# Longformer attention fused with a feed-forward layer: units 16 to 127 issued by one function, attention two units later, twelve more units by seven products of halves

## The chip, the core and the metric

The kernel runs on one core of a Trainium2 chip. The metric is the device time of one execution in microseconds (us), as the median of several runs; less is better. TensorE (PE) multiplies matrices and writes PSUM; VectorE (DVE), ScalarE (ACT) and GpSimd (POOL) do elementwise work, and the SyncE queue (SP) issues the DMAs. Each of these engines takes its instructions in the order in which they stand in its queue.

## The reference

There are 8 batches with 8 heads; each head has 512 local and 32 global tokens of 64 numbers. Local tokens attend to a band of 32 to each side and to the global tokens; global tokens attend to all. The result, 4608 rows of 512, goes through a feed-forward layer with 2048 hidden values:

```
s_l = concat(scale * q_l @ k_g.T, where(|i - j| <= 32, scale * q_l @ k_l.T, -1e9))
out_l = softmax(s_l) @ concat(v_g, v_l)
out_g = softmax(scale * q_g @ concat(k_g, k_l).T) @ concat(v_g, v_l)
x = concat(out_g, out_l).reshape(4608, 512)
h = x @ w_in                                            # 512 -> 2048
y = (max(h, 0) + alpha * min(h, 0)) @ w_out             # 2048 -> 512
```

The attention's inputs are float32; w_in and w_out are float64, and the kernel decodes their bits.

## The kernel before, in words

**Units.** The feed-forward layer is cut into units. Unit T = 16 G + f takes batch G (512 rows; G = 8 is the batch of all global rows) and 128 hidden values, f = 0 to 15. Its first half (`f1`, line 804) makes h, 128 hidden by 512 rows, in a PSUM bank `h_ps`; the slopes follow on DVE and ACT (`slopes`, line 903, or `negatives` and `add_slopes`, lines 887 and 892); the result is split into an upper part gh (ACT) and a lower part gl (POOL). Its second half (`f2`, line 919) adds 12 products of 128x512 to the four banks o0 to o3. `f2` of a unit is issued two units later (LAG = 2). Each number is the sum of two parts (xh and xl, two planes of a weight), and three of the four products of parts are made.

**Plain and fast units.** A plain unit's h takes 12 matmuls over 512 columns. `f1_fast` (line 831) makes two units together by seven products of halves, each of 6 matmuls over 256 columns: 4 products in the even unit (of the x parts b11, t1, t2, t3, in this order), 3 in the odd one (b22, b21, t4). It needs sums of quarters of the weights (`weight_sums`, line 396: per pair of units q, 6 DVE subtractions and additions, 3 ACT copies, 3 POOL subtractions into s24, s3 and a quarter of the weights), and sums of quarters of x (`x_sums`, line 735, called by `prepare`, line 791, at the places that X_STEPS names): for b11, t1, t2, t3, b22, b21 and t4 an upper part by ACT and a lower part by DVE or POOL, and between them subtractions `less` (line 732) in x_raw. In `product` (line 825) the third matmul of the first half reads the lower part of x.

**Attention.** It runs beside the units in quarters of four for each pair of heads P (four pairs are a batch). In the quarter s = 0 PE makes the local scores (`s_ps`), DVE masks and reduces them, ACT takes the exponentials, POOL multiplies by the inverse sums (`p`). In s = 1 and s = 3 DVE transposes and the SP queue sends p through a scratch buffer in DRAM. In s = 2 PE makes the weighted values of the pair before (`o_ps`, then `g_ps`) and the global scores (in `g_ps`), ACT copies the values to x_raw, and the global softmax follows. DVE clears a part of the g_ps bank (MEMSET, line 560) before PE may write it. The x sums of a batch need its four pairs.

**Stages.** `begin` (line 996) issues units 0 to 15, the decoding of the weights and the first pairs by a planner. Units 16 to 29 (`slow_unit`, line 1171) leave the order on DVE, ACT and POOL to the framework's scheduler; units 30 and 31 (`border_units`) and 32 to 127 (`fast_unit`, line 1216) keep the order in which they are written. Units 0 to 31 and 128 to 143 are plain, 32 to 127 fast. On PE all is in written order. In `fast_unit` a unit t has the quarter s = (t + 22) mod 4.

Of the kernel before, what the change touches and what calls it, by code (L numbers as in the profile page):

```python
# [34 lines left out]
HP = 50  # L35
NPRE = 19
LAG = 2
# [265 lines left out]
def longformer_ffn(ctx: ExitStack, tc: tile.TileContext, qk, v, w, alpha, out):  # L303
# [82 lines left out]
    def load_out_weights(T):  # L386
        wos[T] = wpool.tile([128, 2, 512], F32R, tag="w", name="wo")
        sync.dma_start(wos[T].bitcast(F32), wod[T % NF])
# [342 lines left out]

    def less(o, a, b):
        vec.tensor_tensor(o, a, b, op=ALU.subtract)

    def x_sums(G, step):
        if step == 0:
            upper(G, "b11", b11)
            lower(G, "b11", b11, vec)
            less(b11, b12, b11)
        if step == 1:  # L740
            less(b12, b22, b12)
        if step == 2:
            upper(G, "t1", b11)
            upper(G, "t3", b12)
            lower(G, "t1", b11, vec)
        if step == 3:
            less(b11, b22, b11)
            upper(G, "t2", b11)
# [13 lines left out]
    def x_last(step):  # L762

        G = NB - 1
        if step == 0:
            upper(G, "b11", b11)
            lower(G, "b11", b11, vec)
            less(b11, b12, b11)
            less(b12, b22, b12)
        if step == 1:  # L770
            spare("t2")
            upper(G, "t1", b11)
            upper(G, "t3", b12)
            lower(G, "t1", b11, vec)
        if step == 2:
            less(b11, b22, b11)
            lower(G, "t3", b12, vec)
        if step == 3:
            upper(G, "t2", b11)
            upper(G, "b22", b22)  # L780
            upper(G, "b21", b21)
            lower(G, "t2", b11, vec)
        if step == 4:
            lower(G, "b22", b22, pool)
            lower(G, "b21", b21, vec)
        if step == 5:
            less(b21, b21, b11)
            upper(G, "t4", b21)
            lower(G, "t4", b21, pool)

    def prepare(t, at):
        G, f = divmod(t, NF)
        if f:
            G += 1
        if G == NB - 1 and (f, at) in LAST_STEPS:
            x_last(LAST_STEPS.index((f, at)))
        if G * NF not in FAST or (f, at) not in X_STEPS:
            return
        if G < NB - 1:
            x_sums(G, X_STEPS.index((f, at)))  # L800
# [24 lines left out]
    def product(dst, w, x, start):  # L825
        for c in range(2):
            for j, e in ((0, 0), (1, 0), (0, 1)):
                matmul(dst, w[:, j, 128 * c : 128 * c + 128], x[e][:, 256 * c : 256 * c + 256], start=start, stop=not start, skip_group_check=True)
                start = False

    def f1_fast(T):
        G, f = divmod(T, NF)
        q = f // 2
# [49 lines left out]
        if f == NF - 1:  # L883
            return added, both
        return even, odd

# [5 lines left out]
    def add_slopes(T, g, h):  # L892
        f = T % NF
# [9 lines left out]
    def slopes(T, h, n):  # L903
        f = T % NF
# [73 lines left out]

    def values(P, first):
        last = gpart.pop(P)  # L980
        if live(P - 1):
            ob = bank(first, "o_ps")
            pv_all(P - 1, ob, last)
        if live(P):
            global_scores(P)
        if live(P - 1):
            pv_out(P - 1, ob, last)
# [127 lines left out]
    def attn(u, where):  # L1115
        P, s = divmod(u, 4)
        if not (live(P) or live(P - 1)):
            return
        if (s, where) == (0, "pre") and live(P):
            local_scores(P)  # L1120
        if s < 2 and where == "pre" and live(P):
            part = softmax(P, s)
            part["red"]()
            part["ex"]()
            tails.extend(part[k] for k in ("rza", "rzr", "nm"))
        if where == "mid":
            while tails:
                tails.pop(0)()
        if (s, where) == (2, "mid"):
            gpart[P] = global_bank(P)  # L1130
            values(P, "s")
            if live(P):
                load_v(P)
        if not live(P):
            return
        if (s, where) == (2, "post"):
            global_softmax(P)
            if live(P + 2):
                load_qk(P + 2)
        if P >= NRAW:  # L1140
            if (s, where) == (2, "pre") and (P, 0) not in scratch:
                transpose_q(P, 0)
            if u == NPRE + 2 * NF + len(CATCH) - 1 and where == "post":
                transpose_q(P, 0)
            if (s, where) == (3, "pre") and P > 8:
                fetch_pt(P, 0)
                transpose_q(P, 1)
            if (s, where) == (3, "post") and P > 8:
                fetch_pt(P, 1)

    tails = []

    begin()
    pin_sync[0] = False
    steps = [[] for t in range(NT + LAG)]
    u = NPRE + NF
    for t in range(NF, NT + LAG):
        steps[t] = [u, u + 1] if t in CATCH else [u]
        u = steps[t][-1] + 1

    def attention(t, at):
# [189 lines left out]
```

## Time and profile before

| | us |
|---|---|
| median of three runs | 886.47 (884.85 to 890.36) |
| the profiled execution, as timed | 887.61 |
| its span (first to last instruction) | 885.8 |
| around the span | 1.8 |
| PE busy in the span | 866.2 |
| DVE, ACT, POOL busy | 616.3, 392.7, 323.9 |

The times in the rows below count from the start of the span. A row of the timeline gives the start, how long it lasts until its last instruction ends, engine, line, operation, the tiles (out<-in), shapes, the number of instructions, and in brackets idle time before it with what ended it. A matmul's end is modelled; starts of matmuls that follow each other give their pace.

### The profile page before, as it was taken

The numbers are of one execution on the slowest core, as the hardware profiler recorded it, in microseconds if no ns is written. First come the engines' busy times: TensorE is split into PE (matmuls) and PEld (weight loads), VectorE is DVE, ScalarE is ACT, GpSimd is POOL, SyncE is SP. The second block draws the span as 40 slices with busy tenths as digits, with TensorE's granted clock in tenths as the row PEclk, the third lists the DMA queues.
The fourth block names the chain that finished last, engine by engine and source line by source line (L and its number), as shares of the span: only waits on it lengthen the run. The fifth ranks groups of instructions, "written<-read, shape, count | busy, mean of one in ns | idle before, by whom it ended". The sixth has DMA issues, their size and how long they took to land.

```text
span 885.8 us, 22467 instructions
## 1 busy us (share of the span) xinstructions
PE 866.2 (98%) x8678; PEld 751.2 (85%) x8678; DVE 616.3 (70%) x1690; ACT 392.7 (44%) x1162; POOL 323.9 (37%) x281
## 2 busy tenths in 40 slices
PE   7799999999999999999999999999999999999998
PEld 5677777878888888888898888888898898889898
DVE  7999999976767667666676667666676656455432
ACT  7898885544444334432354334432354324211221
POOL 4455443655434332423243332423243323222222
PEclk9999999999999999999999999999999999999999
DMA  9879997977457766776657666776657553645630
GB/s 357 343 256 387 335 336 251 324 247 236 152 180 220 250 214 220 263 241 232 211 173 254 211 215 217 255 250 231 212 184 250 173 185 95 215 168 169 220 134 25
DMA packets 80906, 201.23 MB, mean 227 GB/s; under 512 B 21280, under 2 KB 41248, under 8 KB 77088
## 3 DMA queue, kind: packets, MB, share of 16 engines
q1 hardware_dynamic: 80800, 199.80, 66.1%
q8 instruction: 69, 1.13, 0.5%
q14 instruction: 37, 0.30, 0.1%
HBM read 160.96 MB, written 38.80 MB: 226 GB/s over the span
## 4 chain that ended last, share of the span: by engine, by line
PE 73%; DVE 14%; DMA 6%; ACT 4%; issue 2%; POOL 1%; SPq 1%; DVEq 0%; ACTq 0%; POOLq 0%
PE o L323 34%; PE h_ps L323 30%; PE o_ps L323 4%; PE s_ps L323 3%; DVE wt L294 2%; PE g_ps L323 2%; DVE wsum L294 2%; DVE p L294 2%; DVE g L294 2%; ACT p L294 2%; DVE wraw L294 1%; DMA pt<-scratch 1%; DMA scratch<-p 1%; DMA v<-in_v_dram 1%; DMA wa<-wt 1%
## 5 line engine op out<-in xcount | busy, mean ns | idle before, releaser
L294 POOL TENSOR_TENSOR gl<-g,gh 128x512 fp32r<-128x512 f32 (+1 forms) x128 | 161.4, 1263 | 368.0 <-ACT gh L294 270.4
L323 PE MATMUL o<-gh,wo 128*128 128x512 f32 (+1 forms) x1024 | 244.4, 380 | 0.0
L323 PE MATMUL h_ps<-xh,wt 128*128 128x256 f32 (+1 forms) x1024 | 222.4, 310 | 2.2 <-DVE g L294 1.3
L294 ACT CAST gh<-g 128x512 fp32r<-128x512 f32 (+1 forms) x144 | 85.9, 597 | 289.0 <-DVE g L294 288.3
L323 PEld LDWEIGHTS o<-gh,wo 128*128 128x128 f32 x1024 | 176.7, 188 | 32.1 <-issue 0.4
L323 PEld LDWEIGHTS h_ps<-xh,wt 128*128 128x128 f32 x1024 | 166.2, 188 | 20.5 <-issue 4.0
L323 PE MATMUL h_ps<-xl,wt 128*128 128x256 f32 (+1 forms) x512 | 157.4, 307 | 0.0
L323 PE MATMUL o<-gl,wo 128*128 128x512 f32 (+1 forms) x512 | 131.2, 377 | 0.0
L294 DVE TENSOR_SCALAR g<-h_ps,alpha_sb 128x512 f32<-128x512 f32 (+1 forms) x116 | 82.5, 712 | 39.0 <-PE h_ps L323 33.6
L323 PEld LDWEIGHTS o<-gl,wo 128*128 128x128 f32 x512 | 92.8, 188 | 18.5
L294 POOL TENSOR_TENSOR p<-p,rz 128x512 f32<-128x512 f32 x64 | 70.7, 1121 | 96.2 <-DVE rz L294 93.4
L323 PEld LDWEIGHTS h_ps<-xl,wt 128*128 128x128 f32 x512 | 96.1, 188 | 5.1
L294 DVE TENSOR_TENSOR h_ps<-u,h_ps 128x256 f32<-128x256 f32 x144 | 61.1, 425 | 50.6 <-PE h_ps L323 48.7
L294 ACT ACTIVATE p<-p,mn 128x128 f32<-128x128 f32 x224 | 86.9, 396 | 5.1 <-DVE mn L294 4.9
L323 PE MATMUL h_ps<-xh,s 128*128 128x256 f32 x480 | 88.6, 280 | 0.4 <-DVE h_ps L294 0.2
L294 DVE TENSOR_TENSOR u<-u,h_ps 128x256 f32<-128x256 f32 x96 | 40.3, 420 | 57.0 <-PE h_ps L323 36.7
L323 PEld LDWEIGHTS h_ps<-xh,s 128*128 128x128 f32 x480 | 75.9, 188 | 4.3 <-ACT xe L294 0.7
L294 DVE SCALAR_TENSOR_TENSOR g<-h_ps,g 128x512 f32<-128x512 f32 (+1 forms) x116 | 75.9, 654 | 3.8
L323 PE MATMUL h_ps<-xl,s 128*128 128x256 f32 x240 | 67.1, 279 | 0.0
L294 POOL TENSOR_TENSOR wt<-wt,wr 128x512 int32<-128x512 int32 x32 | 45.4, 1423 | 52.4 <-DVE wt L294 35.0
L323 PEld LDWEIGHTS o_ps<-pt,v 128*64 128x64 f32 x1600 | 49.7, 138 | 8.2 <-issue 2.7
L323 PE MATMUL o_ps<-pt,v 128*64 128x32 f32 (+1 forms) x1600 | 53.5, 223 | 1.7 <-DMA pt<-scratch 1.0
(102 smaller groups left out, 1137.1 us busy)
## 6 DMA issues: line engine op xcount, KB each, us to landing
wo<-wo SPq DMA_DIRECT2D x128, 512.0 KB, 4.3
v<-in_v_dram SPq DMA_DIRECT2D x29, 1024.0 KB, 5.4
qk<-in_qk_dram SPq DMA_DIRECT2D x30, 672.0 KB, 7.0
wraw<-in_w_dram SPq DMA_DIRECT2D x32, 512.0 KB, 8.4
scratch<-p SPq DMA_DIRECT2D x112, 128.0 KB, 2.8
pt<-scratch SPq DMA_DIRECT2D x28, 512.0 KB, 5.7
wo<-wt SPq DMA_DIRECT2D x16, 512.0 KB, 7.1
out_dram<-ost SPq DMA_DIRECT2D x32, 256.0 KB, 3.5
```

The costliest lines, as they stand in the source:

```text
L294: ins = op(*a, **k)
L323: ins = nc.tensor.matmul(*a, **k)
```

## The change

Units 16 to 127 are now all issued by one function, `unit`, with the order on DVE, ACT and POOL as it is written; `slow_unit`, `border_units`, the queue of attention steps and `x_last` are gone. The quarter of unit t is s = (t + 20) mod 4, so that attention stands two units further behind: scores are in units 0, 4, 8 and 12 of a batch (before: 2, 6, 10, 14), weighted values in 2, 6, 10 and 14 (before: 0, 4, 8, 12). Units 16 to 19 are plain, 20 to 31 now fast. The x parts of batch 1 are made in units 16, 17 and 20 (`x_second`), with the upper and lower parts of batch 1's x that were there already used as b11, b21, b22 and t4's store. Weight sums are made in two parts, in the units that FIRSTS and RESTS name; pairs q = 0 and 1 come last, and batch 2 takes its hidden values in a turned order (`hidden`). Odd units of batches 1 and 2 use `added` and `both` (negatives on ACT). The last batch uses the same `x_sums` as the others.

```diff
-FAST = range(2 * NF, NB * NF)
-CATCH = (16, 23, 30)
+PLAIN = NF + 4
+FIRSTS = {17: 2, 19: 3, 21: 4, 23: 5, 25: 6, 27: 7, 33: 0, 37: 1}
+RESTS = {18: 2, 20: 3, 22: 4, 24: 5, 26: 6, 28: 7, 34: 0, 38: 1}
 X_STEPS = [(12, "mid"), (13, "post"), (14, "post"), (15, "pre"), (15, "mid"), (15, "post"), (0, "mid")]
-LAST_STEPS = [(12, "post"), (13, "mid"), (13, "post"), (14, "mid"), (14, "post"), (15, "mid")]
+LATE = 4
+    def x_second(step):
+        if step == 0:
+            less(b11, b12, b11)
+            less(b12, b22, b12)
+            upper(1, "t1", b11)
+            upper(1, "t3", b12)
+        if step == 1:
+            ...
+            lower(1, "t1", b11, vec)
+            less(b11, b22, b11)
+            upper(1, "t2", b11)
+            lower(1, "t3", b12, vec)
+            less(b21, b21, b11)
+            lower(1, "t2", b11, vec)
+        if step == 2:
+            for c in range(2):
+                act.copy(xs[1, "t4"](0, c), x_raw[:, 2 + c, 0:256])
+                pool.tensor_tensor(xs[1, "t4"](1, c), x_raw[:, 2 + c, 0:256], xs[1, "t4"](0, c).bitcast(F32), op=ALU.subtract)
     def x_sums(G, step):
         if step == 0:
             upper(G, "b11", b11)
             lower(G, "b11", b11, vec)
+        if step == 1:
             less(b11, b12, b11)
-        if step == 1:
-            less(b12, b22, b12)
+            one_half(b12, b22, b12, 0)
         if step == 2:
             upper(G, "t1", b11)
+            lower(G, "t1", b11, vec)
+            one_half(b12, b22, b12, 1)
+            less(b11, b22, b11)
+        if step == 3:
+            if G == NB - 1:
+                spare("t2")
             upper(G, "t3", b12)
-            lower(G, "t1", b11, vec)
-        if step == 3:
-            less(b11, b22, b11)
             upper(G, "t2", b11)
         if step == 4:
             lower(G, "t2", b11, vec)
+    def hidden(T):
+        G, f = divmod(T, NF)
+        return (f + LATE) % NF if G == 2 else f
-        if f == NF - 1:
+        if f == NF - 1 or G in (1, 2):
             return added, both
-    def fast_unit(t):
-        P, s = divmod(steps[t][0], 4)
+    def unit(t):
+        P, s = divmod(t + 20, 4)
...
-        one, two = f1_fast(t)
+        one, two = f1_plain(t) if t < PLAIN else f1_fast(t)
...
+            if t == NF:
+                x_second(0)
+            if t == PLAIN:
+                x_second(2)
+            if t in RESTS and s == 0:
+                late.pop(RESTS[t])()
             prepare(t, "mid")
...
+            if t == NF + 1:
+                x_second(1)
             prepare(t, "mid")
             if s == 1 and live(P):
                 transpose_q(P, 0)
...
+            if t in FIRSTS:
+                late[FIRSTS[t]] = weight_sums(FIRSTS[t], True)
         f2(t - LAG, 0)
...
         f2(t - LAG, 1)
+        if t in RESTS and s == 2:
+            late.pop(RESTS[t])()
-        if NF <= t < 2 * NF and t % 2 == 0:
-            store_a21((t - NF) // 2)
+        if NF <= t < NF + NF // 2:
+            store_a21((2, 3, 4, 5, 6, 7, 0, 1)[t - NF])
```

Three places of the order that results. The first is PE where batch 3 begins, after the product of t3 in unit 48 (s_2854 before, s_3984 after are tiles of weight sums). Before, the weighted values of a pair follow it:

```order
L323 MATMUL h_ps<-xh,s_2854 128x256 x2
L323 MATMUL h_ps<-xl,s_2854 128x256
L323 MATMUL o_ps<-pt,v 64x32 x2
L323 MATMUL o_ps<-pt,v 64x2x32 x2
L323 MATMUL o_ps<-pt,v 64x32 x4
L323 MATMUL o_ps<-pt,v 64x2x32 x2
```

After, the out-projection follows, and then unit 49 (s_3983):

```order
L322 MATMUL h_ps<-xh,s_3984 128x256 x2
L322 MATMUL h_ps<-xl,s_3984 128x256
L322 MATMUL o_3945<-gh,wo 128x512 x2
L322 MATMUL o_3946<-gh,wo 128x512 x2
L322 MATMUL o_3947<-gh,wo 128x512 x2
L322 MATMUL o_3948<-gh,wo 128x512 x2
L322 MATMUL o_3945<-gl,wo 128x512
L322 MATMUL o_3946<-gl,wo 128x512
L322 MATMUL o_3947<-gl,wo 128x512
L322 MATMUL o_3948<-gl,wo 128x512
L322 MATMUL h_ps<-xh,s_3983 128x256 x2
L322 MATMUL h_ps<-xl,s_3983 128x256
```

The weighted values moved out of the stretch between the even and the odd products of the first pair of units of a batch; the scores moved in ahead of that stretch.

The second is DVE at the same border. Before, from the softmax of unit 46 (rz) to the subtraction that makes t4 in unit 48 (the last row), with the lower parts of t3, t2, b21 among the xl rows and the MEMSET for unit 48:

```order
L294 RECIPROCAL rz<-rz 128x4 x2
L294 TENSOR_TENSOR xl<-x_raw,xh 128x512
L294 TENSOR_TENSOR h_ps<-u,h_ps 128x256 x2
L294 TENSOR_TENSOR x_raw<-x_raw 128x2x256
L294 SCALAR_TENSOR_TENSOR g<-g,beta_sb,h_ps 128x512 x2
L294 TENSOR_TENSOR xl<-x_raw,xh 128x512 x2
L294 STREAM_TRANSPOSE p<-p 128x512 x2
L294 MEMSET g_ps 64x32
L294 TENSOR_TENSOR u<-u,h_ps 128x256 x2
L294 TENSOR_TENSOR h_ps<-u,h_ps 128x256
L294 TENSOR_TENSOR xl<-x_raw,xh 128x512
L294 TENSOR_TENSOR x_raw<-x_raw 128x2x256
```

After, the stretch of units 46 and 47, from the global softmax to the lower parts of t2 and t3:

```order
L293 TENSOR_TENSOR x_glb<-x_glb,g_ps 128x32
L293 TENSOR_REDUCE gm<-g_ps 128x1
L293 TENSOR_SCALAR gm<-gm 64x1 x2
L293 TENSOR_SCALAR gz<-gz 64x1 x2
L293 RECIPROCAL gz<-gz 128x1
L293 TENSOR_TENSOR xl<-x_raw,xh 128x512
L293 TENSOR_TENSOR x_raw<-x_raw 128x256
L293 TENSOR_TENSOR x_raw<-x_raw 128x2x256
L293 STREAM_TRANSPOSE sg_sb<-sg_sb 128x384
L293 TENSOR_TENSOR h_ps<-u,h_ps 128x256 x2
L293 SCALAR_TENSOR_TENSOR g<-g,beta_sb,h_ps 128x512 x2
L293 TENSOR_TENSOR xl<-x_raw,xh 128x512 x2
```

Eight masked reductions of the scores of unit 48 follow, and then:

```order
L293 ISA p,mn<-s_ps,mask 128x4x32
L293 ISA mn 128x1
L293 TENSOR_TENSOR u<-u,h_ps 128x256 x2
L293 TENSOR_TENSOR h_ps<-u,h_ps 128x256
L293 TENSOR_TENSOR xl<-x_raw,xh 128x512
L293 TENSOR_TENSOR x_raw<-x_raw 128x2x256
L293 RECIPROCAL rz<-rz 128x4 x2
```

The global softmax stands ahead of the lower part of t1, and eight reductions stand between the lower part of t3 and the sums u; the subtraction for t4 stands behind them.

The third is DVE in units 16 to 18. Before, the MEMSET for unit 18 stands among the weight sums of one pair (wsum) in unit 16 or 17 (the g rows are the slopes):

```order
L294 TENSOR_TENSOR wsum<-wsum 128x256
L294 MEMSET g_ps 64x32
L294 TENSOR_TENSOR wsum<-wsum 128x256 x3
L294 TENSOR_SCALAR g<-h_ps,alpha_sb 128x512
L294 TENSOR_TENSOR wsum<-wt 128x512 x2
L294 SCALAR_TENSOR_TENSOR g<-h_ps,g 128x512
L294 RECIPROCAL rz<-rz 128x4 x2
L294 TENSOR_TENSOR wsum<-wsum 128x256 x4
L294 STREAM_TRANSPOSE p<-p 128x512 x2
```

After, it stands behind the slopes of units 16 and 17, the x sums of batch 1, the transposes of p and the first weight sums:

```order
L293 SCALAR_TENSOR_TENSOR g<-g,beta_sb,h_ps 128x512
L293 TENSOR_TENSOR x_raw<-x_raw 128x2x256 x2
L293 RECIPROCAL rz<-rz 128x4 x2
L293 SCALAR_TENSOR_TENSOR g<-g,beta_sb,h_ps 128x512
L293 TENSOR_TENSOR xl<-x_raw,xh 128x512
L293 TENSOR_TENSOR x_raw<-x_raw 128x2x256
L293 TENSOR_TENSOR xl<-x_raw,xh 128x512
L293 TENSOR_TENSOR x_raw<-x_raw 128x2x256
L293 TENSOR_TENSOR xl<-x_raw,xh 128x512
L293 STREAM_TRANSPOSE p<-p 128x512 x2
L293 TENSOR_TENSOR wsum<-wt 128x512 x2
L293 MEMSET g_ps 64x32
```

The MEMSET moved from ahead of the second weight sum to behind all x sums of batch 1 and the transposes.

## Rows read from the trace of the kernel before

**Rows 1.** The profile's page: the span, and busy time, share and instructions of each engine.
```profile
span 885.8 us, 22467 instructions
PE 866.2 (98%) x8678; PEld 751.2 (85%) x8678; DVE 616.3 (70%) x1690; ACT 392.7 (44%) x1162; POOL 323.9 (37%) x281
```

**Rows 2.** The timeline of PE: where the out-projection (`f2`) begins in units 20, 21, 36, 38, 54, 114 and 116.
```profile
177.55 1.99 PE L323 MATMUL o<-gh,wo 128*128 128x512 f32 x8
183.04 1.99 PE L323 MATMUL o<-gh,wo 128*128 128x512 f32 x8
...
285.12 2.12 PE L323 MATMUL o<-gh,wo 128*128 128x512 f32 x8
...
296.99 1.31 PE L323 MATMUL o<-gh,wo 128*128 128x512 f32 x5
...
396.56 1.76 PE L323 MATMUL o<-gh,wo 128*128 128x512 f32 x7
...
763.25 1.99 PE L323 MATMUL o<-gh,wo 128*128 128x512 f32 x8
...
773.62 1.76 PE L323 MATMUL o<-gh,wo 128*128 128x512 f32 x7
```

**Rows 3.** The timeline of PE: three rows that began late, with what ended the wait.
```profile
147.39 0.74 PE L323 MATMUL h_ps<-xh,wt 128*128 128x512 f32 x2 [0.56 <-DVE g L294]
...
284.02 0.69 PE L323 MATMUL g_ps<-pt,v 128*64 128x32 f32 x16 [0.69 <-DVE g_ps L294]
...
745.22 0.48 PE L323 MATMUL h_ps<-xh,s 128*128 128x256 f32 x2 [0.25 <-DVE h_ps L294]
```

**Rows 4.** The timeline of all engines in unit 44: the values and the global softmax. The products of unit 44 begin in the first row, those of unit 45 in the second; the third is ACT's product with the inverse sums.
```profile
329.50 0.40 PE L323 MATMUL h_ps<-xh,wt 128*128 128x256 f32 x2
...
337.78 0.40 PE L323 MATMUL h_ps<-xh,s 128*128 128x256 f32 x2
337.86 0.62 ACT L294 ACTIVATE sg_sb<-sg_sb,gz 128x384 f32<-128x384 f32 x1 [0.76 <-DVE gz L294]
```

**Rows 5.** The timeline of all engines in units 46 to 49, around the border to batch 3: scores of unit 46, its products and first sums, unit 47's products, sums, slopes and the lower parts of t2 and t3, then unit 48's products, values, lower part of b21, the subtraction for t4, its upper (ACT) and lower part (POOL).
```profile
342.75 1.16 PE L323 MATMUL s_ps<-qk 64*32 64x128 f32 x64
...
343.84 0.50 PE L323 MATMUL h_ps<-xh,wt 128*128 128x256 f32 x2
343.95 0.29 DVE L294 CUSTOM_DVE_ANT_0 p<-s_ps,mask 128x128 f32<-128x128 f32 x1
...
347.05 0.88 DVE L294 TENSOR_TENSOR u<-u,h_ps 128x256 f32<-128x256 f32 x2 [1.32 <-ACT p L294]
...
349.52 0.40 PE L323 MATMUL h_ps<-xh,s 128*128 128x256 f32 x2
...
351.17 0.41 DVE L294 TENSOR_TENSOR h_ps<-u,h_ps 128x256 f32<-128x256 f32 x1
...
352.78 1.40 DVE L294 SCALAR_TENSOR_TENSOR g<-g,beta_sb,h_ps 128x512 f32<-128x512 f32 x2
...
354.10 2.39 DVE L294 TENSOR_TENSOR xl<-x_raw,xh 128x512 fp32r<-128x512 f32 x2
...
354.25 3.38 POOL L294 TENSOR_TENSOR gl<-g,gh 128x512 fp32r<-128x512 f32 x2 [2.11 <-ACT gh L294]
354.39 0.40 PE L323 MATMUL h_ps<-xh,wt 128*128 128x256 f32 x2
...
358.72 0.67 PE L323 MATMUL g_ps<-pt,v 128*64 128x32 f32 x16
...
359.73 0.69 DVE L294 TENSOR_TENSOR x_raw<-x_raw 128x512 f32<-128x512 f32 x1
...
360.45 0.62 ACT L294 CAST xh<-x_raw 128x512 fp32r<-128x512 f32 x1 [4.08 <-DVE x_raw L294]
...
361.15 1.30 POOL L294 TENSOR_TENSOR xl<-x_raw,xh 128x512 fp32r<-128x512 f32 x1 [2.28 <-ACT xh L294]
```

**Rows 6.** The timeline of DVE, then of PE, at the same border: the lower part of t3 by itself, the transposes of p, the lower part of b21; then the begin of unit 49's products and the first matmul there that reads the lower part of t4.
```profile
354.70 1.79 DVE L294 TENSOR_TENSOR xl<-x_raw,xh 128x512 fp32r<-128x512 f32 x1
356.41 1.29 DVE L294 STREAM_TRANSPOSE p<-p 128x512 f32<-128x512 f32 x2
...
359.01 0.68 DVE L294 TENSOR_TENSOR xl<-x_raw,xh 128x512 fp32r<-128x512 f32 x1
...
362.67 0.40 PE L323 MATMUL h_ps<-xh,s 128*128 128x256 f32 x2
...
364.32 0.28 PE L323 MATMUL h_ps<-xl,wt 128*128 128x256 f32 x1
```

**Rows 7.** The timeline of DVE and PE in units 16 to 18: the lower parts gl with which `begin` ends, the values of unit 18.
```profile
150.38 1.28 DVE L294 TENSOR_TENSOR gl<-g,gh 128x512 fp32r<-128x512 f32 x2
...
162.66 1.59 PE L323 MATMUL o_ps<-pt,v 128*64 128x32 f32 x48
...
164.08 0.66 PE L323 MATMUL g_ps<-pt,v 128*64 128x32 f32 x16
```

**Rows 8.** Groups by line and shape over the whole span: count, busy us, mean ns of one, and idle time before.
```profile
L294 POOL TENSOR_TENSOR p<-p,rz 128x512 f32<-128x512 f32 x64 | 70.7, 1121 | 96.2 <-DVE rz L294 93.4 <-DVE mn L294 2.0 <-ACT sg_sb L294 0.4
...
L294 DVE TENSOR_TENSOR wsum<-wt 128x512 f32<-128x512 f32 x16 | 13.8, 900 | 1.3 <-PE o L323 1.3
...
L294 POOL TENSOR_TENSOR s<-wsum,s 128x512 fp32r<-128x512 f32 x8 | 11.2, 1402 | 7.5 <-ACT s L294 7.4
```

More of the change, by code (lines that the diff above doesn't have):

```diff
@@ L794, in prepare @@
             G += 1
[L795 to L799, printed above, removed]
+        if 2 <= G < NB and (f, at) in X_STEPS:
             x_sums(G, X_STEPS.index((f, at)))
@@ L881, in both, with f1_plain, half, whole @@
                 lower_g(T - 1 + i, g, SL)
-        if f == NF - 1:
+        if f == NF - 1 or G in (1, 2):
             return added, both
         return even, odd
+    def f1_plain(T):
+        h = f1(T, True)
+        def half():
+            us["below"] = negatives(h)
+        def whole():
+            g = us.pop("below")
+            add_slopes(T, g, h)
+            upper_g(T, g, SL)
+            lower_g(T, g, SL)
+        return half, whole
     def negatives(h):
@@ L903, in slopes @@
     def slopes(T, h, n):
-        f = T % NF
+        f = hidden(T)
         g = stage("g")
@@ L977, in longformer_ffn @@
     gpart = {}
[L979 to L987, printed above, removed]
     def values_pe(P):
@@ L1113, in begin @@
             issue(name)
[L1115 to L1149, printed above, removed]
@@ L1151, in longformer_ffn @@
-    tails = []
     begin()
     pin_sync[0] = False
[L1155 to L1161, printed above, removed]
-        with tc.high_priority(offset=HP):
-            if len(steps[t]) == 1:
-                attn(steps[t][0], at)
-                return
-            order = [(k, a) for k in range(2) for a in ("pre", "mid", "post")]
-            i = 2 * ("pre", "mid", "post").index(at)
-            for k, a in order[i : i + 2]:
-                attn(steps[t][k], a)
@@ L1171, in slow_unit @@
-    def slow_unit(t):
-        attention(t, "pre")
-        if t < NT:
-            f1(t)
-        attention(t, "mid")
-        f2(t - LAG, 0)
-        attention(t, "post")
-        prepare(t, "mid")
-        f2(t - LAG, 1)
-    def border_units(t):
-        if t == 2 * NF - 2:
-            u, v = steps[t]
-            P, s = divmod(v, 4)
-            assert s == 0 and live(P)
-            attn(u, "pre")
-            attn(u, "mid")
-            f1(t)
-            attn(u, "post")
-            local_scores(P)
-            parts = waiting[P] = [softmax(P, h) for h in range(2)]
-            parts[0]["red"]()
-            parts[1]["red"]()
-            f2(t - LAG, 0)
-            f2(t - LAG, 1)
-            parts[0]["ex"]()
-            return
-        P = steps[t][0] // 4
-        parts = waiting.pop(P)
-        prepare(t, "pre")
-        parts[1]["ex"]()
-        f1(t)
-        for part in parts:
-            part["rza"]()
-        f2(t - LAG, 0)
-        prepare(t, "mid")
-        for part in parts:
-            part["rzr"]()
-            part["nm"]()
-        gpart[P] = global_bank(P)
-        f2(t - LAG, 1)
@@ L1264, in fast_unit @@
         f2(t - LAG, 1)
+        if t in RESTS and s == 2:
+            late.pop(RESTS[t])()
+    late = {}
     load_out_weights(NF)
```

69 lines of the change are left out of this document (18 added, 51 removed).

## The prediction

> **What bounds the kernel now.** I read the page first: PE is busy for 866.2 of 885.8 us and DVE for 616.3 [rows 1]. The reader is to see that the end is set by PE's own queue, so that a microsecond counts only if it makes PE's work shorter or makes PE wait. I read next where the out-projection begins in successive units. A plain unit takes 183.04 - 177.55 = 5.49, a plain pair 10.98. A fast pair without attention takes 773.62 - 763.25 = 10.37 [rows 2]. A fast batch with all of its attention takes 396.56 - 296.99 = 99.57 [rows 2], and the starts in it leave no gap at the border of batches. Third came the waits of PE, which are small: 0.56 where `begin` ends, up to 0.69 for a MEMSET in batch 1, 0.25 near the end [rows 3]. Last came the timeline of all engines around a border, since the diff moves work there [rows 4 to 6].
>
> **Twelve more units by seven products.** They are six pairs: 6 x (10.98 - 10.37) = 3.7 off PE's own work. To see what else batch 1 can give, I hold its 16 units against a steady batch: 285.12 - 177.55 = 107.57, against 99.57 [rows 2], 8.0 more. Of that, 2.7 isn't to be had: this stretch holds the values of one pair more than a window of the new order would, and such values cost what a product's begin is delayed by them, 362.67 - 354.39 = 8.28 with values against 349.52 - 343.84 = 5.68 without [rows 5, 6], so 2.6 to 2.7. What is left is 5.3: the 3.7, and 1.6 of small waits such as the one of 0.69 [rows 3] which the scheduled order has and a steady batch has not. I take **+5.3**. The wait of 0.25 and its like near unit 111 go with the separate handling of the last batch: I take **+0.5**, with 0.25 as the lower end.
>
> The Trainium skill speaks against this part: TensorE: Matmul & The Clock Gate, Back-to-back issue gap, has matmuls in a stream follow each other in about 81 ns at 128 columns and 131 ns at 512, so that halves cost more than half. By an estimate between the two (98 ns at 256 columns), 42 matmuls of a fast pair would take 4.1 us against 3.1 us for 24 plain ones, and the six pairs would lose 6 us; the sum would then come out near 904. The trace disagrees: its fast pair is 0.61 shorter than its plain one [rows 2], and the measurement decides.
>
> **Units 16 to 18.** The scores now stand ahead of unit 16's products and fill the wait of 0.56 [rows 3], so PE would come to the global part (g_ps) of unit 18 at 164.08 - 0.56 = 163.5 [rows 7]. What it needs there is the MEMSET, which moved on DVE behind the x sums of batch 1. DVE's chain: the lower parts gl end at 150.38 + 1.28 = 151.66 [rows 7]; eight reductions take 1.78 (343.95 to 347.05 - 1.32) [rows 5]; slopes of unit 16 0.7, two subtractions 1.4, which gives 155.5. The slopes of unit 17 need its products: one plain unit of 5.49 and half of another behind 147.9, so 156.1, and then ACT's negatives, which stand behind exponentials and two copies of x; I let them begin at 157.7. Then 0.7 of slopes, five subtractions of x at 0.68 (3.4), two transposes 1.29 [rows 6], two weight sums of 0.90 [rows 8]: 164.9. That is **-1.4**. It would be -0.4 if the slopes begin at once behind 156.7, and -2.9 if POOL holds up two of the subtractions as it does the lower part of t3, 1.79 instead of 0.68 [rows 6].
>
> **Units 20 to 28.** In units 20, 24 and 28 POOL now makes three sums of weights ahead of p: one of 1.40 [rows 8] and two of half its size, some 2.8. Count from the scores' begin S. In the rows p can end at S + 9.2 at the soonest (the sums u, an inverse, and 2 x 1.12) [rows 5, 8], and at the latest at S + 13.7, where its transposes begin (356.41 - 342.75) [rows 5, 6]. With 2.8 these are 12.0 and 16.5; I take the middle, 14.3. The transposes (1.29) and two weight sums (1.80) follow on DVE, so the MEMSET comes at S + 17.4. PE wants it at 358.72 - 342.75 = S + 16.0 [rows 5]: late by 1.4 in unit 22. In unit 26 no parts of x (two of about 0.65) stand ahead on POOL, which leaves 0.1 to 1.4: I take 0.5. In unit 30 no weight sums stand between, and nothing is lost. Sum **-1.9**, from 0 to -3.6 (p at its latest in unit 22).
>
> **The borders of batches 2 to 6** (units 32, 48, 64, 80, 96) carry the sum. Before, they lose nothing: the values lie between the even and the odd products of the border pair, so PE asks for the lower part of t4 only at 364.32, and POOL has it at 361.15 + 1.30 = 362.45 [rows 5, 6]. After, the values stand two units earlier, the scores stand ahead of the pair, and eight reductions come between the lower part of t3 and the first sums u. I count from the products of the pair's predecessor (unit 46 after is built as unit 44 before).
> - ACT ends the global softmax at 337.86 + 0.62 - 329.50 = 8.98 [rows 4]. Then, on ACT and DVE: copy of t1 0.62, its lower part 0.68, subtractions 0.41 and 0.69, the transpose of sg at most 0.65 (half of 1.29): 12.0, where unit 47's first sum can begin. PE's products for it would have let it begin at 8.28 + 351.17 - 349.52 = 9.9 [rows 4, 5], so DVE is late by 2.1.
> - From this sum to the lower part of t2 are 354.10 - 351.17 = 2.93 [rows 5]. (A subtraction leaves that stretch, two copies on ACT of 0.62 enter it; I keep the figure.) The lower parts of t2 and t3 take 2.39 [rows 5], in which POOL's gl holds t3's at 1.79 instead of 0.68 [rows 6]. End: 17.3.
> - PE has the scores at 342.75 - 329.50 = 13.25, the even products at 14.34 [rows 4, 5]. t3 is the fourth of four products of six matmuls, and its lower part is asked for by the 21st matmul: at the pace of 1.65 for 14 (362.67 to 364.32) [rows 6], 2.36 later, at 16.7. PE waits **0.65**.
> - DVE goes on: reductions 1.78, three sums 1.29, the lower part of b21 0.68: 21.1. From the subtraction for t4 to the end of its lower part on POOL 362.45 - 359.73 = 2.72 [rows 5]: 23.8. PE begins the odd products at 14.34 + 0.65 + 5.68, asks for that part 1.65 later, at 22.3, and waits **1.5**.
>
> So 2.15 for each border. Without POOL's hold on t3's part DVE is 1.11 earlier: 1.0. The trace shows that hold [rows 6], so I take 1.9, close to the former: 5 x 1.9 = **-9.5**. The ends are 0.4 (no hold, no transpose in the way) and 3.3 (the lower part of b21 held too, + 1.1). A gain is excluded, since nothing is lost there before. At the last border (unit 112) no attention is left: u waits for PE's four products (about 3.0), then 1.29 + 0.68 + 2.72 = 7.7, against 5.68 + 1.65 = 7.3: 0.4, or 1.5 with one hold; I take **-0.9**.
>
> On that hold the Trainium skill says (SBUF — State Buffer, SBUF: two separate sides) that VectorE and GpSimd share one pair of ports, locked for a whole instruction, so that the later one stands still. The trace agrees: the same subtraction takes 0.68 alone and 1.79 beside POOL's gl [rows 6]. By it alone the border would be 2.15 and the sum 1.5 worse.
>
> **Sum.** +5.3 + 0.5 - 1.4 - 1.9 - 9.5 - 0.9 = -7.9. The profiled execution took 887.6 and lies 1.1 above the median of 886.5; 887.6 + 7.9 = 895.5 there, 894.4 as a median. The queue of DMA loads I cost at nothing: they are asked for a unit or more ahead of their use, as before; a load that came late would be seen as PE waiting for pt or v.
>
> **Rivals.**
> 1. The borders are hidden: the transposed sg or the reductions find gaps and t3, t4 come in time. For it speaks that no border loses anything now; against it that t4's last 2.72 can't begin before the reductions are through. Then only +5.3 + 0.5 - 1.4 - 1.9 = +2.5 remains: 884.0, on the other side.
> 2. Nothing waits: the MEMSETs are early as well, and the 0.56 is gained: 5.8 + 0.56 = 6.4, 880.1. For it speaks DVE's load of 70% [rows 1], against it the order, which puts the MEMSET behind more work in units 18, 22 and 26.
> 3. POOL also holds the lower part of b21 at every border: 5 x 3.25 and 1.5 at the last, 5.8 - 1.4 - 1.9 - 16.3 - 1.5 = -15.3: 901.8. The gl of two units (3.38) [rows 5] begins near where b21 stands; against it, by then it should be over.
>
> **How the numbers follow.** Forecast 0.52, with a range of its own from 887 to 900 (1.0 or 2.5 for each border, the other terms between their ends); first rival 0.18, second 0.10, third 0.20. The second and the third reach to the ends, so the range is 881 to 901. One per cent, 8.9 us, is about what a measurement of this kernel can tell from no change: slower than 895.3 are the third rival and somewhat under half of the forecast, 0.41 in all; faster than 877.6 is only the second with more waits of batch 1 gone than I see, 0.04; within 1% is the rest, 0.55.
>
> **What would show it.** In the profile after, PE's timeline should show, at the first pair of each batch from 2 on, a wait of about 0.6 for DVE's xl in the even unit and of about 1.5 for POOL's xl in the odd one; in units 18 and 22 a wait for DVE before g_ps; pairs of batch 1 without attention at 10.37; no wait of 0.56 at the end of `begin`. The step that would make the forecast wrong is the chain from the global softmax to t4: if DVE's first reduction of unit 48 begins when its scores are ready, the border costs nothing and the kernel is faster than before; if the lower part of b21 takes 1.8, it is slower than forecast.

## The result: slower by 0.8%

The changed kernel takes 892.99 us (median of 8 runs, 892.04 to 897.51), the kernel before 886.81 in the same runs: a ratio of 1.0077, with a 95% interval from 1.0058 to 1.0096. That is 6 to 7 us more. The forecast was 894.4, with a range from 881 to 901. Sign and size are right; two terms of the sum are not, and they err in opposite directions.

**The profile after.** The page, to be held against [rows 1]: PE has 1.5 us more of busy time in a span that is 6.9 longer, so most of what was added is idle time of PE.

```profile
span 892.7 us, 22793 instructions
PE 867.7 (97%) x8786; PEld 756.9 (85%) x8786; DVE 613.8 (69%) x1703; ACT 413.5 (46%) x1203; POOL 321.8 (36%) x283
```

The view of PE's waits (what waited, for what; us in total, times, longest) names two releasers that the kernel before hardly had:

```profile
PE h_ps L322 <- POOL xl L293: 4.6, 6, 0.9
PE g_ps L322 <- DVE g_ps L293: 4.3, 4, 2.3
```

The first is the lower part of t4 at the six borders, the second the MEMSET of the g_ps bank in units 18, 22, 26 and 30; the largest wait of that kind before was 0.69 [rows 3].

**Units 18, 22, 26.** PE's timeline of the changed kernel:

```profile
162.74 1.59 PE L322 MATMUL o_ps<-pt,v 128*64 128x32 f32 x48
166.61 0.69 PE L322 MATMUL g_ps<-pt,v 128*64 128x32 f32 x16 [2.28 <-DVE g_ps L293]
...
167.71 3.52 PE L322 MATMUL o<-gh,wo 128*128 128x512 f32 x8
171.03 1.28 PE L322 MATMUL o<-gl,wo 128*128 128x512 f32 x4
172.15 0.62 PE L322 MATMUL h_ps<-xh,wt 128*128 128x512 f32 x2
...
194.89 0.69 PE L322 MATMUL g_ps<-pt,v 128*64 128x32 f32 x16 [0.99 <-DVE g_ps L293]
...
220.36 0.69 PE L322 MATMUL g_ps<-pt,v 128*64 128x32 f32 x16 [0.67 <-DVE g_ps L293]
```

The reader is to see two costs in the first stop: 2.28 of idle time, and behind it eight matmuls that last 3.52 where others last 1.99 [rows 2]. The view by stretches (busy us of each engine, then PE's granted clock, DMA share, GB/s) says why:

```profile
164.00:166.60 2.60, 0.33 (x12) 0.22 (x8) 2.60 (x7) 0.26 (x1) 0.00 (x0) 1.00 0.85 303
...
168.00:170.00 2.00, 2.00 (x6) 1.57 (x6) 1.17 (x5) 0.78 (x4) 1.21 (x1) 0.51 1.03 217
170.00:172.00 2.00, 2.00 (x7) 1.53 (x7) 1.70 (x6) 0.77 (x3) 0.00 (x0) 0.64 1.00 369
```

PE had worked 0.33 of 2.60 us; then its granted clock was 0.51, the level of 1.2 GHz, before it rose again. Twelve matmuls took 172.15 - 167.71 = 4.44 instead of 12 x 0.229 = 2.75. The stop cost 2.28 + 1.7 = 4.0.

The timeline of DVE and POOL ahead of the stop shows why DVE comes to the MEMSET so late:

```profile
159.74 1.41 DVE L293 TENSOR_TENSOR x_raw<-x_raw 128x512 f32<-128x512 f32 x1
160.57 1.75 POOL L293 TENSOR_TENSOR gl<-g,gh 128x512 fp32r<-128x512 f32 x1
161.08 1.79 DVE L293 TENSOR_TENSOR xl<-x_raw,xh 128x512 fp32r<-128x512 f32 x1
...
166.47 0.09 DVE L293 MEMSET g_ps<- 64x32 f32 x1
```

Two of the x sums that stand ahead of it last 1.41 and 1.79 beside POOL's work, where 0.68 each is usual [rows 6]. That is 1.8 of the delay.

**The border at unit 48.** All engines, in order of time, to be held against [rows 5, 6]:

```profile
342.17 0.39 PE L322 MATMUL h_ps<-xh,wt 128*128 128x256 f32 x2
...
351.48 0.69 DVE L293 TENSOR_TENSOR xl<-x_raw,xh 128x512 fp32r<-128x512 f32 x1 [1.25 <-ACT xh L293]
...
353.52 0.73 DVE L293 TENSOR_TENSOR h_ps<-u,h_ps 128x256 f32<-128x256 f32 x2
...
356.10 2.41 DVE L293 TENSOR_TENSOR xl<-x_raw,xh 128x512 fp32r<-128x512 f32 x2
...
356.31 0.51 PE L322 MATMUL h_ps<-xh,wt 128*128 128x256 f32 x2
...
356.67 3.00 POOL L293 TENSOR_TENSOR gl<-g,gh 128x512 fp32r<-128x512 f32 x2 [11.97 <-ACT gh L293]
...
358.44 0.28 DVE L293 CUSTOM_DVE_ANT_0 p<-s_ps,mask 128x128 f32<-128x128 f32 x1
...
358.77 0.28 PE L322 MATMUL h_ps<-xl,s 128*128 128x256 f32 x1
...
360.12 0.86 DVE L293 TENSOR_TENSOR u<-u,h_ps 128x256 f32<-128x256 f32 x2
...
361.02 0.43 DVE L293 TENSOR_TENSOR h_ps<-u,h_ps 128x256 f32<-128x256 f32 x1
...
362.00 0.40 PE L322 MATMUL h_ps<-xh,s 128*128 128x256 f32 x2
...
362.08 0.69 DVE L293 TENSOR_TENSOR x_raw<-x_raw 128x512 f32<-128x512 f32 x1
...
363.50 1.27 POOL L293 TENSOR_TENSOR xl<-x_raw,xh 128x512 fp32r<-128x512 f32 x1 [2.58 <-ACT xh L293]
364.83 0.38 PE L322 MATMUL h_ps<-xl,wt 128*128 128x256 f32 x1 [0.84 <-POOL xl L293]
```

DVE's reductions begin at 358.44, behind the lower part of t3, 2.1 after the products of unit 48 began (356.31), which stand behind the scores in PE's queue. The lower part of t3 is ready 0.3 before PE reads it (358.77), and that of t4 too late. From the begin of the odd products (362.00) and 1.65 for 14 matmuls [rows 6], PE would have read it at 363.7; it did at 364.83, so a border costs 1.1.

**Ahead of unit 16 and behind unit 114.** Three rows of PE's timeline. The out-projection of unit 13 begins, up to which PE's order is the same in both kernels, in the kernel before and in the changed one; then the out-projection in unit 114 begins, in a second profile of the changed kernel (experiment 11). The latter row is at 763.25 before [rows 2] and at 767.80 in the first profile after (it stands with the pairs in the section on the forecast).

```profile
141.18 2.00 PE L323 MATMUL o<-gh,wt 128*128 128x512 f32 x8
```

```profile
142.12 1.99 PE L322 MATMUL o<-gh,wt 128*128 128x512 f32 x8
```

```profile
770.58 2.00 PE L322 MATMUL o<-gh,wo 128*128 128x512 f32 x8
```

The first profile after was 0.9 late before PE came to anything that the change moved. By unit 114 it was 4.5 late, the second one 7.3. Their spans are 6.9 and 7.4 longer than before, so the first lost 2.4 more behind unit 114, where no attention is left, and the second almost nothing. Experiments 8 and 11 look into this.

### The profile page after: what moved, and what is told of

Read it like the earlier page. It is cut to its first block, busy times and chain, and to the rows that moved or that the text cites. A ratio compares the mean times of both kernels' runs of the same rounds, so it can differ in the third digit from the quotient of the medians.

```text
span 892.7 us, 22793 instructions
## 1 busy us (share of the span) xinstructions
PE 867.7 (97%) x8786; PEld 756.9 (85%) x8786; DVE 613.8 (69%) x1703; ACT 413.5 (46%) x1203; POOL 321.8 (36%) x283
## 4 chain that ended last, share of the span: by engine, by line
PE 66%; DVE 13%; issue 8%; ACT 5%; POOL 4%; DMA 3%; SPq 1%; POOLq 0%; DVEq 0%; ACTq 0%
PE o L322 31%; PE h_ps L322 27%; PE o_ps L322 3%; PE s_ps L322 3%; DVE wt L293 2%; PE g_ps L322 2%; ACT p L293 2%; DVE g L293 2%; POOL gl L293 2%; DVE p L293 2%; POOL xl L293 2%; DMA pt<-scratch 2%; DVE wraw L293 1%; DMA scratch<-p 1%; DVE xl L293 1%
## 5 line engine op out<-in xcount | busy, mean ns | idle before, releaser
L322 PE MATMUL h_ps<-xh,wt 128*128 128x256 f32 (+1 forms) x1024 | 210.0, 300 | 2.0 <-DVE g L293 1.0
L322 PE MATMUL h_ps<-xl,wt 128*128 128x256 f32 (+1 forms) x512 | 152.1, 297 | 4.6 <-POOL xl L293 4.6
L293 DVE TENSOR_TENSOR h_ps<-u,h_ps 128x256 f32<-128x256 f32 x162 | 68.0, 425 | 57.7 <-PE h_ps L322 55.5
L322 PE MATMUL h_ps<-xh,s 128*128 128x256 f32 x552 | 100.0, 278 | 0.0
L322 PEld LDWEIGHTS h_ps<-xh,s 128*128 128x128 f32 x552 | 87.0, 188 | 3.8
L293 DVE TENSOR_SCALAR g<-h_ps,alpha_sb 128x512 f32<-128x512 f32 (+1 forms) x86 | 60.3, 702 | 37.1 <-PE h_ps L322 33.3
L293 DVE TENSOR_TENSOR u<-u,h_ps 128x256 f32<-128x256 f32 x108 | 45.3, 420 | 56.0 <-PE h_ps L322 49.3
L322 PE MATMUL h_ps<-xl,s 128*128 128x256 f32 x276 | 76.6, 278 | 0.0
L293 DVE CUSTOM_DVE_ANT_0 p<-s_ps,mask 128x128 f32<-128x128 f32 x224 | 49.6, 285 | 14.2 <-PE s_ps L322 13.4
L293 DVE SCALAR_TENSOR_TENSOR g<-h_ps,g 128x512 f32<-128x512 f32 (+1 forms) x86 | 55.2, 642 | 3.0
```

Source lines behind the costliest of these rows:

```text
L293: ins = op(*a, **k)
L322: ins = nc.tensor.matmul(*a, **k)
```

## The experiments

All are edits of the changed kernel. Ratios are against the kernel before in the same runs, as the changed kernel's 1.0077.

**1. The MEMSET in the odd unit.**

```diff
-        if s == 2 and (live(P) or live(P - 1)):
-            gpart[P] = global_bank(P)
...
                 transpose_q(P, 1)
+            if s == 1 and (live(P) or live(P - 1)):
+                gpart[P] = global_bank(P)
             one()
```

> The changed kernel with one edit: the MEMSET of the g_ps bank stands at the begin of the odd unit (17, 21, 25, 29, ...), ahead of the x sums and weight sums there, instead of at the begin of the next even unit. Theory (PE waits for a MEMSET that stands behind other DVE work): the waits of g_ps in units 18, 22, 26 and 30 (2.28, 0.99, 0.67 and about 0.4 in the profile of the changed kernel) go, and so does the slow stretch of matmuls behind the first of them (twelve of 0.43 instead of 0.23, some 2.4 us): 6 to 7 us less, about 886.5. Rival (DVE has too much to do in batch 1, and its lateness only moves): PE then waits in units 18 to 30 for something else that DVE makes, the transposed p or the sums u, and under 2 us are won, over 891.

Measured: 889.87, ratio 1.0040 (1.0017 to 1.0063). No wait for the MEMSET is left and the granted clock stays at 1.00 between 160 and 176. Of the 6 to 7 us only 3 to 4 came, because in unit 28 a new wait appeared:

```profile
232.92 0.62 ACT L293 CAST xh<-x_raw 128x512 fp32r<-128x512 f32 x1
233.57 0.75 DVE L293 TENSOR_TENSOR xl<-x_raw,xh 128x512 fp32r<-128x512 f32 x1 [1.82 <-ACT xh L293]
...
236.72 0.48 PE L322 MATMUL h_ps<-xh,wt 128*128 128x256 f32 x2 [1.40 <-DVE g L293]
```

ACT makes the upper part of b11 behind its copies of weight sums, DVE waits 1.82 for it, and PE's next products wait for the slopes behind that, since they need the same PSUM banks. The earlier waits had covered most of it. The theory was right about the waits that go, the rival that a part of the lateness moves; neither had the size.

**2. and 3. t4's chain ahead of the reductions**, alone and with the first edit.

```diff
             upper(G, "b21", b21)
-        if step == 6:
             lower(G, "b21", b21, vec)
```

(and the sixth step's place, unit 0 of the batch, struck from X_STEPS)

> The changed kernel with one edit: at a border of batches the lower part of b21, the subtraction for t4 and t4's two parts are issued at the end of the unit before the border, ahead of the scores' reductions, instead of behind them. Theory (t4's chain stands behind the reductions): the six waits of PE for t4's lower part (0.84 each in the view of waits, 1.25 by the starts of the matmuls) go, 6 us less, about 887. Rival (the exponentials that come 1.4 later make p, its way through DRAM or the sums u late): the borders lose as much elsewhere, and the time stays over 891. Second rival (t4 hangs on POOL, which is busy with gl and the lower part of b22, not on the reductions): PE still waits for POOL's xl at half the size or more, 890 or above.

> Both edits of the two kernels before in the changed kernel. Theory: the two costs are apart from each other and add up: 12 to 13 us less than the changed kernel, about 880.5, which is some 6 us less than the kernel before. Rival (an engine's load is the bound): less than the better of the two edits alone plus 2 us.

Measured: 907.79, ratio 1.0230 (1.0198 to 1.0262), and with the first edit 902.16, ratio 1.0166. This fell flat: the first is 15 us slower than the changed kernel, not 6 us faster, over 891 as its first rival had it. The border to batch 3 in it:

```profile
359.50 4.11 DVE L293 TENSOR_TENSOR xl<-x_raw,xh 128x512 fp32r<-128x512 f32 x3
...
363.02 1.74 POOL L293 TENSOR_TENSOR xl<-x_raw,xh 128x512 fp32r<-128x512 f32 x1
363.64 1.67 DVE L293 TENSOR_TENSOR x_raw<-x_raw 128x512 f32<-128x512 f32 x1
...
366.92 0.86 DVE L293 TENSOR_TENSOR u<-u,h_ps 128x256 f32<-128x256 f32 x2
...
368.40 0.47 PE L322 MATMUL h_ps<-xh,s 128*128 128x256 f32 x2 [2.75 <-DVE h_ps L293]
```

Two things are to be seen. Three lower parts last 4.11 and the subtraction 1.67, where 0.69 each is usual: DVE meets POOL's gl and lower part of b22 (1.74) on the way. And the odd products wait for the sums u (2.75 here, 16.2 at the six borders), which read the PSUM halves that these products overwrite. In the changed kernel the sums are done 0.55 before PE wants to go on (361.45 and 362.00). So the order of the changed kernel, t4 behind the sums u, is the better one; the reductions are in t4's way, but the sums u are more urgent.

Some of these stops cost more than the wait. The view by stretches has the stop at the border to batch 4 and what follows it, then the same for the border to batch 5:

```profile
466.50:469.70 3.20, 0.62 (x3) 0.19 (x1) 3.13 (x20) 2.79 (x13) 1.27 (x1) 1.00 0.62 208
469.70:473.00 3.30, 3.04 (x14) 3.07 (x15) 0.54 (x4) 1.42 (x9) 1.73 (x2) 0.51 0.04 14
569.70:572.70 3.00, 0.51 (x3) 0.07 (x1) 2.93 (x20) 2.71 (x12) 1.27 (x1) 1.00 0.49 161
572.70:576.00 3.30, 2.96 (x22) 2.87 (x23) 1.76 (x6) 1.50 (x10) 1.65 (x2) 1.00 0.05 17
```

Behind the first the granted clock was 0.51, the level of 1.2 GHz, and behind the second, of nearly the same length, it stayed at 1.00. Of the six stops three were followed by the slow clock.

**4. Units 20 to 31 plain, with both edits.**

```diff
-        one, two = f1_plain(t) if t < PLAIN else f1_fast(t)
+        one, two = f1_plain(t) if t < 2 * NF else f1_fast(t)
```

(the calls of `x_second` are gone; the plain units read weights of which a quarter is replaced by then)

> The kernel with both edits, but units 20 to 31 plain again and without the x sums for batch 1 (weight sums, order and attention stay). By the theory that a fast pair saves 0.61 of PE's work and waits for nothing here, it is slower than the kernel with both edits by 6 x 0.61 = 3.7 us. If the fast units of batch 1 cost DVE and ACT time that PE waits for, it is slower by less than 2 us, or faster. If halves cost more than half, as the notes on the gap between matmuls have it, it is faster by some 6 us.

Measured: 901.96, no different from 902.16. It tells little: without the fast units the wait in unit 28 (1.3) and most of that in unit 33 (3.0, now 0.75) went too, which makes up for 3.7. It was done again as 10.

**5. t4's lower part by DVE.**

```diff
-            lower(G, "t4", b21, pool)
+            lower(G, "t4", b21, vec)
```

> The changed kernel with the lower part of t4 at the borders made by DVE instead of POOL, in the same place. In its profile ACT has the upper part at 363.43 in unit 48, POOL the lower at 364.77 and PE wants it at 363.7. Theory (the last step of the chain sets the wait): DVE needs 0.68 instead of 1.27, so PE waits some 0.6 less at each of six borders: 3.5 us less, about 889.5. Rival (DVE is late already, so a further instruction there delays its next sums and slopes): PE waits for DVE instead, 892 to 895.

Measured: 889.08, ratio 1.0027 (1.0015 to 1.0040), some 4 us less than the changed kernel, as expected. At the border to batch 3:

```profile
363.47 0.69 DVE L293 TENSOR_TENSOR xl<-x_raw,xh 128x512 fp32r<-128x512 f32 x1 [0.69 <-ACT xh L293]
...
364.22 0.39 PE L322 MATMUL h_ps<-xl,wt 128*128 128x256 f32 x1 [0.22 <-DVE xl L293]
```

PE reads t4's lower part 0.6 sooner, and DVE, which had waited 0.69 for PE there, loses little. This shows that the wait at the border hangs on t4's chain.

**6. and 7. t1's step ahead of the global softmax**, alone, and with the MEMSET, DVE for t4, and ACT's copy for b11 earlier in unit 28.

```diff
-X_STEPS = [(12, "mid"), (13, "post"), (14, "post"), ...
+X_STEPS = [(12, "mid"), (13, "post"), (14, "mid"), ...
```

> The changed kernel with one step of the x sums earlier: the upper and lower part of t1, half a subtraction and the one for t2 stand ahead of the global softmax of unit 14 of a batch (of 46, 62, ...) instead of behind it, where DVE had waited 1.25 for ACT's copy, which stood behind the softmax. Theory (the whole border hangs on DVE's chain from there: sums, slopes, lower parts, reductions, u, b21, t4): the chain begins 0.7 to 0.8 earlier, and PE's wait for t4 shrinks from 0.84 to 0.1 to 0.2 at each border of batches 2 to 6: 3 to 4 us less, about 889.5. Rival (the border hangs on the reductions of the scores, which can't come before their scores, or on POOL): no less than 891.5. Second rival (the global softmax, now 1 us later, makes its transposes and the parts of p late): over 894.

> The changed kernel with four edits: the MEMSET in the odd unit, t1's step ahead of the global softmax, t4's lower part on DVE, and ACT's copy for b11 of batch 2 in unit 28 ahead of the copies of the weight sums (there the first of these edits alone had left DVE waiting 1.82 for that copy, and PE 1.4 for the slopes behind it). Theory: no wait of PE over 0.3 is left from unit 16 on, 10 to 11 us less than the changed kernel, about 882, so some 5 us less than the kernel before. Rival (the costs hide each other, and the next instruction in DVE's queue is late): 886 or more.

In both, the step's subtractions read two of the four pairs of heads of a batch before the last values are there, so t2, t3 and t4 are other numbers. Measured: 894.53 (ratio 1.0091, 1.0065 to 1.0116) and 880.70 (0.9936, 0.9913 to 0.9959). Alone the step brings nothing, as its first rival had it (no less than 891.5): PE's waits for POOL's xl fall from 4.6 to 4.0, because the sums u then wait for PE's even products instead. The four together bring 12 us, somewhat more than the 10 to 11 expected.

**8. and 11. The pace of the halves**: one matmul of 64 columns more at unit 110, and the changed kernel once more.

```diff
+        if t == 110:
+            matmul(bank("s", "s_ps")[:, 0:64], wts[0, 0][:, 0, 0:128], wts[0, 0][:, 1, 0:64], start=True, stop=True)
```

> The changed kernel with one matmul more on PE, 64 columns of weights into a free bank at the begin of unit 110; nothing else. The profile of the kernel before has its halves of 256 columns 0.1133 apart from unit 110 on, the changed kernel 0.118, which is 2.3 us over the last 34 units, at the same granted clock. Theory (two ways in which PE's weight loads and matmuls can stand to each other, kept until something disturbs them, and an odd matmul is enough): from unit 110 on the halves follow each other in 0.1133, 2.3 us less, about 890.7. Rival (the pace depends on where tiles lie, or on what else the memory does): unchanged, 893 to 894.

> The changed kernel once more, word for word, for a second profile. Question: is the pace of halves in the last units (0.118 in the first profile, 0.1133 with one more matmul) the program's or the run's? If it is the program's, units 112 on take 121.1 again, and one matmul more flips it; if it is the run's, they take 118.7 in some profile, and the run with one more matmul showed nothing. The waits for MEMSET and t4 should be the same as in the first profile within 0.1.

Measured: 892.87 and 895.40 (ratios 1.0075 and 1.0080). With one matmul more the tail did run at the faster pace, but so did the second profile of the unaltered program. Begins of the products of two successive units near the end, in the kernel before, the changed kernel, and its second profile:

```profile
868.47 0.39 PE L323 MATMUL h_ps<-xh,wt 128*128 128x256 f32 x2
...
871.19 0.39 PE L323 MATMUL h_ps<-xh,a 128*128 128x256 f32 x2
```

```profile
866.37 0.40 PE L322 MATMUL h_ps<-xh,a 128*128 128x256 f32 x2
...
869.20 0.40 PE L322 MATMUL h_ps<-xh,wt 128*128 128x256 f32 x2
```

```profile
867.64 0.39 PE L322 MATMUL h_ps<-xh,a 128*128 128x256 f32 x2
...
870.36 0.39 PE L322 MATMUL h_ps<-xh,wt 128*128 128x256 f32 x2
```

24 matmuls take 2.72, 2.83 and 2.72. The pace is not fixed by the program, since the same program has either in two runs, and the extra matmul showed nothing. The waits were the same in both profiles: 4.6 and 4.7 for POOL's xl, 4.3 and 4.4 for the MEMSET.

**9. and 10. Three edits** (MEMSET, DVE for t4, b11's copy ahead of the sums' copies in unit 28), and the same with units 20 to 31 plain.

```diff
+            if t == 28:
+                upper(2, "b11", b11)
             if t in RESTS and s == 0:
                 late.pop(RESTS[t])()
```

> The changed kernel with three edits: the MEMSET in the odd unit, t4's lower part on DVE, and ACT's copy for b11 of batch 2 ahead of the copies of the weight sums in unit 28. Unlike the kernel with four edits it leaves t1's step where it was, so that its sums of x are those of the reference. Theory (the waits are apart from each other, and t1's step gave only 0.2 for each border): what the kernel with four edits took, 880.7, and 1 more: 881.5 to 882, some 5 us less than the kernel before. Rival (t1's step carried a good part of the gain): 884 or more.

> The kernel with three edits, but with units 20 to 31 plain and without the x sums of batch 1; the weight sums stay, and the plain units read weights of which a quarter is replaced by then, so they compute other values. Theory (a fast pair saves 0.61 of PE's work, and with these edits hardly anything waits in batch 1): 3.7 us more than the kernel with three edits. Rival (the fast units' work on DVE and ACT costs PE as much as it saves): within 1.5 us of it, or less.

Measured: 885.19, ratio 0.9971 (0.9959 to 0.9984), and 887.29, ratio 1.0000 (0.9983 to 1.0018). The first is above the 881.5 to 882 expected and where the rival had it (884 or more): t1's step carried a part of the gain, as 12 bears out. The three edits are worth 9 us against the changed kernel by the ratios, 8 by the medians, which is more than the change had lost. The six fast pairs are worth 2.1 us by the medians and 2.6 by the ratios, between the theory's 3.7 and the rival's 1.5; the intervals of the two ratios are too wide to rule out either. In the profile with three edits PE still waits in unit 21 and at the five borders of batches 2 to 6:

```profile
PE h_ps L322 <- DVE xl L293: 1.5, 6, 0.4
```

**12. The three edits and t1's two parts alone ahead of the softmax.**

```diff
+        if 2 <= G < NB and (f, at) == (14, "mid"):
+            upper(G, "t1", b11)
+            lower(G, "t1", b11, vec)
...
-            upper(G, "t1", b11)
-            lower(G, "t1", b11, vec)
             one_half(b12, b22, b12, 1)
```

> The kernel with three edits (885.2) and, as a fourth, t1's upper and lower part alone ahead of the global softmax of unit 14 of a batch; the subtractions that read the batch's last values stay behind it, so the sums of x are those of the reference. In the kernel with three edits PE still waits 0.39 for t4 at each border and 0.57 in unit 32. Theory (the border hangs on DVE's chain, which t1's step delays): the six waits shrink to about 0.2 or less and that of unit 32 to half, 1.5 us less, about 883.7. Rival (no wait of PE that can be told from noise hangs on it): 885 to 886. If the pace of the halves follows the place of this step rather than the run, the time comes near the 880.7 of the kernel with four edits.

Measured: 878.98 (878.35 to 880.10), ratio 0.9931 (0.9917 to 0.9944), the fastest version by its median (experiment 7, 0.9936, lies within its interval). That wait is down to

```profile
PE h_ps L322 <- DVE xl L293: 0.2, 1, 0.2
```

and the first sum of unit 47 waits for PE, which it did not in the changed kernel (353.52, with no wait in front):

```profile
343.71 0.43 DVE L293 TENSOR_TENSOR h_ps<-u,h_ps 128x256 f32<-128x256 f32 x1 [0.26 <-PE h_ps L322]
```

So the border did hang on DVE's chain from t1 on, but only once t4's last step was short. The gain over 9 is 0.4 of a per cent by the ratios, 3.5 us, more than the 1.5 expected. The two profiles are 6.6 apart (spans of 883.9 and 877.3): 0.6 of it lies ahead of unit 16, 2.3 are these waits and that of unit 32, and nearly all of the rest is the pace of the halves, whose mean distance in batches 2 to 6 is 0.1172 in one and 0.1158 in the other. Whether t1's place sets that pace, as the last sentence of the expectation has it, stays open: the unaltered changed kernel has 0.1155 in its first profile and 0.1173 in its second, so runs of one program differ as much.

## Why the forecast was right, and where not

- **Bound.** Right: PE's idle time made most of the difference, and the two kinds of stop that cost most were named before with their places and releasers (DVE's MEMSET, POOL's lower part of t4). Of the others, the wait for DVE's xl in the even unit of a border was named and did not come, and that in unit 30 came and was not named.
- **Six pairs and small waits, +5.3 and +0.5.** Nearly right as a whole, 5.5 by the count below, but split otherwise. Experiments 9 and 10 give 2.1 for the pairs, against 3.7. About 0.5 of the difference is the row that was taken: the pair of 10.37 [rows 2] ran at the faster pace of halves, and the same pair in the changed kernel takes 778.26 - 767.80 = 10.46, so that six pairs give 3.1:

```profile
767.80 2.00 PE L322 MATMUL o<-gh,wo 128*128 128x512 f32 x8
...
778.26 2.00 PE L322 MATMUL o<-gh,wo 128*128 128x512 f32 x8
```

  The remainder is what PE waits for even with three edits where the kernel with plain units has no wait, as 0.4 for t4 in unit 21. The spacing in the Trainium skill (TensorE: Matmul & The Clock Gate, Back-to-back issue gap) would, by the prediction's estimate, have made the pairs 6 us dearer; the measurement has them cheaper.
- **Units 16 to 18, -1.4.** This term failed in size: 4.0. The wait was 2.28, within the stated 0.4 to 2.9 but above the value taken: POOL did hold two of the x sums, which the prediction had only for its far end (its own numbers make that end 1.4 + 2 x 1.11 = 3.6, not 2.9). The slow clock behind the stop, 1.7, was not in the sum at all. Nor was the 0.56 that PE gains ahead of unit 16: the term counts the wait from the earlier arrival and credits the gain nowhere.
- **Units 20 to 28, -1.9.** Nearly right: 0.99, 0.67, and some 0.4 in unit 30, where nothing had been expected; about 2.3 by how late the matmuls start.
- **Borders, -9.5.** Too high: 1.1 each, 5.5. The step that failed is PE's wait of 0.65 for t3. From the products of unit 46 the first sum came after 353.52 - 342.17 = 11.35 (12.0 had been reckoned), the lower part of t2 2.58 later (2.93), so that t3 was done at 16.3, not 17.3, and PE asked at 16.6. The hold by POOL was there: 2.41 for the two parts. (With that hold in full at five borders the prediction's sum would have been 5 x 0.25 = 1.25 worse, not 1.5.) All later steps of the chain came 1.0 sooner, and t4's wait was 1.1 instead of 1.5.
- **Last border, -0.9.** 0.6.

With 3.1 for the pairs at the slower pace, about 2.4 for small waits that are gone (five delays of 0.3 to 0.9 that only the kernel before has, those of [rows 3] among them, less one of 0.5 that is new), and -4.0, -2.3, -5.5, -0.6, the sum is -6.9. That this is the very difference of the spans is chance, since it leaves out three parts of the first profile. It was 0.9 late ahead of unit 16, where PE's order is the same; the slower pace of halves cost it 2.4 behind unit 114; and in batches 2 to 6 the mean distance of halves was 0.1155, against 0.1177 in the kernel before, which gave back about 3.4. In the second profile (0.1173 there, and no loss behind unit 114) 1.0 lies ahead of unit 16 and 6.3 between, close to the sum.

The forecast's -7.9 is near by luck in the sizes, though not in the kinds of wait: borders that were reckoned 4.0 too dear made up for 2.6 in units 16 to 18, most of it a slow clock that was not reckoned.

The first rival (hidden borders) would have been true with experiment 12's edits; the third (POOL holds the lower part of b21) did not happen in the changed kernel, as gl was over by then, and did in experiment 2.

## What to carry to other kernels

When work is moved in a kernel that one engine bounds, follow the instruction that this engine waits for through its producer's queue, and ask of each instruction ahead of it whether it is more urgent: the MEMSET of 0.09 us was not held by its own cost but by what stood before it, while the reductions could not be passed without making the more urgent sums late. A wait that is taken away uncovers the next one, so count the gain after all of them are gone. And a sum built on one measured pair inherits the pace at which that pair ran.

## What the hardware showed that was not expected

- After 2.6 us in which PE worked 0.33, its granted clock was 0.51 and then 0.64 over four microseconds at full load; shorter stops (0.99, 0.84) were not followed by such a stretch. Length alone does not settle it: of the six longer stops in experiment 2 three were followed by it and three were not.
- Matmuls of 256 columns have two paces, 0.113 and 0.118, at a granted clock of 1.00 in both. A pace holds over many units and changes at stops and between attention steps, and the same program has either one in the same units of different runs. Over the last 30 units it makes 2.4 us. What selects it was not found, and whether it goes with the single chip that a group of runs had was not tested.
- DVE's subtractions of two SBUF operands take 0.68 alone and 1.67 to 1.8 beside POOL's; the masked reductions of scores, which read PSUM, keep their 0.28 beside POOL's gl (358.44 to 359.67).
